# Attention with decay and two squared-ReLU layers: the opening's scores, decays and exponentials done in another way

## The chip, the cores and the metric

The kernel runs on one core of a Trainium2 chip. The metric is the device time of one execution in microseconds (us), the median of several executions. Five engines work side by side: TensorE (PE; its weight loads are PEld), VectorE (DVE), ScalarE (ACT), GpSimd (POOL), and SyncE (SP), which here issues nearly all transfers.

## The reference

Attention over 4 batches and 8 heads, 576 positions, head size 64, with a decay made from running sums of log f; then two layers without biases, each of width 512 and hidden width 2048, on 2304 tokens.

```python
scores = scale * np.matmul(q, k.transpose(0, 1, 3, 2))          # scale = 1/8
cum = np.cumsum(np.log(np.clip(f, 0.0001, 1.0)), axis=-1)
decay = cum[:, :, :, None] - cum[:, :, None, :]
scores = np.where(causal, -1e9, scores + decay)                 # causal: key after query
attn = np.exp(scores - np.max(scores, axis=-1, keepdims=True))
attn = attn / (np.sum(attn, axis=-1, keepdims=True) + 1e-09)
x = np.matmul(attn, v)                                          # to tokens x 512
x = square(relu(x @ w_in)) @ w_out                              # twice, with weights of their own
```

## The kernel before, in words

**The order of the work.** The program is straight-line code. Every piece of work is registered as `op(engine, duration, function, priority, dependencies, buffers)`, and `Plan.run` plays all of them through once with estimated durations, when the kernel is built. Whenever an engine comes free there, the ready operation of lowest priority number is taken, and it is emitted into that engine's queue at that place. On the chip each engine keeps this order, whatever the real durations are. `either(m, ...)` gives an operation two possible engines: by `m` it prefers one and falls back on the other (0 and 1), or is fixed to one (2 to 4). Where TensorE has nothing to do in the plan, before `wu` = 43.42 us, a filler product (L1442) is emitted; nothing reads its result. The numbers in `TUNE` are priorities and engine choices of this planner, so that a change of them reorders the whole program.

**The stages.** Positions are cut at 0, 64, 192 and so on. The *first part* (`first_part(y, ...)`, y = 0 and 1, two batches each) computes attention for positions 0 to 63; its 256 columns are the first group of tokens (group 0) of the first layer. *Pairs* of heads (`pair`, L644 to L694) do positions 64 to 191, *units* of one head (`unit`, L702 to L830) the rest. The first layer (`hidden`, L918 and L993) goes over groups of 256 tokens and 16 hidden tiles; its 16 weight tiles of 1 MB come in as two words for each number, are decoded on VectorE (L873, L875, L877), rounded on ScalarE (L890) and subtracted for the remainder (L894). The second layer (L1290, L1316) follows.

**The first part before.** One transfer for each y (L530) puts queries and keys of 16 heads into `room[y]`, on 64 partitions, 512 KB. The decay enters as two extra rows of the product: VectorE clips f, ScalarE takes the logarithm, VectorE scans 64 positions (`scan0`) and writes 8 and -8 times the sums (`times8`, L1407) into `a0`; two transfers for each y (L533) then copy these rows to partitions 64 and 65 of `room[y]`. The scores are 16 products of 66 rows for each y (L547). VectorE scales them by 1/8 and adds the mask (L553), takes the maximum (L556), GpSimd or VectorE subtracts it (L557), ScalarE takes one exponential of all 512 columns (L558), VectorE sums (L559), adds 1e-9 (L560), takes the reciprocal (L562), and VectorE or GpSimd multiplies (L563). Then come transposes (L575), a copy (L578), the products with the values (L587), and the split of the result into a rounded part and a remainder (L602, L604), from which group 0 of the first layer starts (L918).

**The transfers' order.** SP issues f, y = 0's queries and keys, the first half of weight tile 0, the decay rows of y = 0, y = 1's queries and keys and its decay rows, the second half of weight tile 0, the values, and weight tiles 1 and 2. All of these except the first three wait for `aug_first`, the end of `scan0`.

Of the kernel before, what the change touches and what calls it, by code (L numbers as in the profile page):

```python
# [19 lines left out]
Q0, QA = QB[1:3]  # L20
# [243 lines left out]
def attention_then_two_squared_relu_mlps(  # L264
# [102 lines left out]
    mask2 = ap_.tile([128, 1, Q0], BF16, name="mask2")  # L367
# [31 lines left out]
    room = [wp.tile([128, 2048], F32, tag="w", name="tmp") for _ in range(9)]  # L399
    WHOLE = Pool([st, ph_a.rearrange("p i n c -> p (i n c)").bitcast(F32)[:, 0:2048], room[3]])  # L400
# [118 lines left out]
    def first_part(y, prio):  # L519

        qk_ = room[y].rearrange("p (n z s) -> p n z s", n=2 * H, z=2)
# [19 lines left out]
        first_loads.extend(l2)  # L541
        l3 = op("SP", P.COPY[0], load_v, U + 4 + y, [aug_first], data=0.95)
# [1046 lines left out]
```

## Time and profile before

| | before |
|---|---|
| median of 3 runs (lowest to highest) | 943.73 us (942.67 to 945.62) |
| profiled execution, its own time | 946.69 us |
| its span in the trace | 944.9 us |
| PE busy | 927.1 us, 98% of the span |
| DVE busy | 694.8 us, 74% |
| ACT busy | 503.5 us, 53% |
| POOL busy | 178.5 us, 19% |
| mean DMA rate | 145 GB/s |

The page gives busy time over the span; it counts the filler products as busy. Durations of matmuls overlap, so that a group's sum can exceed its stretch; busy time of a stretch counts each moment once. The releaser of a wait is the event that came last.

### The profile page before, as it was taken

Reading aid. Unit: us, or ns where it says so; the run is one execution under the profiler, and the core shown is the slowest. Engines: PE = TensorE matmul, PEld = TensorE weight load, DVE = VectorE, ACT = ScalarE, POOL = GpSimd, SP = SyncE. Lnnn points to the kernel's source line nnn. Section 1 sums busy time; section 2 is a strip of 40 time slices with the busy share of each in tenths; the row PEclk is TensorE's granted clock in tenths of the full one; section 3 lists DMA queues with packets and bytes.
Section 4 is the critical chain, followed back from the end, with each engine's and each line's share of the span. In section 5 each row is a group of like instructions: output and inputs, shape, how many; then the busy total and the mean of one; then the engine's idle time right before and its main releaser. Section 6 shows DMA issues by size and latency. Waiting matters only on the chain.

```text
span 944.9 us, 16695 instructions
## 1 busy us (share of the span) xinstructions
PE 927.1 (98%) x6356; PEld 854.5 (90%) x6356; DVE 694.8 (74%) x1363; ACT 503.5 (53%) x1064; POOL 178.5 (19%) x144
## 2 busy tenths in 40 slices
PE   7899999999999999999999999999999999999997
PEld 3899999989999999999999998888989898989886
DVE  7999878888888888786476799896765455745453
ACT  3697799888888998986343662231411012301011
POOL 4021201112112111230101001221821015501010
PEclk7999999999999999999999999999999999999999
DMA  9878458667767757655376229743261211311113
GB/s 271 262 230 253 127 113 180 141 117 171 182 124 173 184 108 155 149 114 112 111 263 218 78 90 292 244 154 134 67 200 68 68 67 67 133 68 67 67 68 112
DMA packets 164288, 137.12 MB, mean 145 GB/s; under 512 B 120752, under 2 KB 140720, under 8 KB 162160
## 3 DMA queue, kind: packets, MB, share of 16 engines
q1 hardware_dynamic: 163952, 135.56, 52.0%
q8 instruction: 50, 0.82, 0.4%
q10 hardware_dynamic: 256, 0.49, 0.2%
q14 instruction: 30, 0.25, 0.1%
HBM read 90.32 MB, written 18.42 MB: 115 GB/s over the span
## 4 chain that ended last, share of the span: by engine, by line
PE 84%; DVE 6%; DMA 4%; ACT 3%; issue 2%; SPq 0%; POOLq 0%; POOL 0%; DVEq 0%; ACTq 0%
PE yp L993 18%; PE hp L918 18%; PE hp L1290 17%; PE bk L1316 13%; PE yp L1316 6%; PE bk L807 4%; PE bk L773 4%; DMA stage<-in_w_dram 2%; PE bk L644 1%; PE bk L683 1%; DMA qk<-aug_d 1%; DVE gt L943 1%; DVE ph L442 1%; PE bk L670 1%; DMA tmp<-tmp 0%
## 5 line engine op out<-in xcount | busy, mean ns | idle before, releaser
L993 PE MATMUL yp<-gt,w 128*128 128x256 f32 x1728 | 229.5, 281 | 0.1
L918 PE MATMUL hp<-xk,w 128*128 128x256 f32 x1728 | 227.3, 282 | 1.6 <-DVE w L894 1.6
L918 PEld LDWEIGHTS hp<-xk,w 128*128 128x128 f32 x1728 | 214.4, 189 | 2.1 <-DVE w L894 1.8
L993 PEld LDWEIGHTS yp<-gt,w 128*128 128x128 f32 x1728 | 214.5, 188 | 0.8 <-DVE gt L943 0.4
L1316 PE MATMUL bk<-w,g 128*128 128x512 f32 x576 | 148.6, 394 | 0.2 <-POOL g L1303 0.2
L1302 ACT CAST g<-r 128x768 fp32r<-128x768 f32 x47 | 39.3, 835 | 181.0 <-DVE r L1301 180.8
L1290 PE MATMUL hp<-w 128*128 128x384 f32 x630 | 124.0, 335 | 0.2
L1316 PEld LDWEIGHTS bk<-w,g 128*128 128x128 f32 x576 | 106.6, 188 | 17.6 <-POOL g L1303 0.6
L1290 PEld LDWEIGHTS hp<-w 128*128 128x128 f32 x630 | 111.8, 188 | 8.2 <-DVE t L1267 0.4
L421 ACT ACTIVATE pp<-pp,stat 128x448 f32<-128x448 f32 (+1 forms) x128 | 78.1, 611 | 11.9 <-DVE stat L413 11.1
L1267 DVE TENSOR_TENSOR r<-hp,st 128x384 f32<-128x384 f32 x62 | 34.5, 556 | 58.2 <-PE hp L1290 58.0
L442 DVE SCALAR_TENSOR_TENSOR ph<-pp,stat,ph 128x320 f16<-128x320 f32 (+2 forms) x96 | 69.0, 722 | 10.2 <-ACT ph L435 9.3
L1303 POOL TENSOR_TENSOR g<-r,g 128x768 fp32r<-128x768 f32 x19 | 35.1, 1848 | 217.5 <-ACT g L1302 217.5
L1290 PE MATMUL hp<-w,far 128*128 128x384 f32 x378 | 74.4, 335 | 0.0
L1316 PE MATMUL yp<-w,g 128*128 128x512 f32 x288 | 74.4, 393 | 0.0
L435 ACT ACTIVATE ph<-pp,stat 128x320 f16<-128x320 f32 (+2 forms) x96 | 63.7, 666 | 16.5 <-DVE stat L429 15.1
L1301 DVE SCALAR_TENSOR_TENSOR r<-r 128x768 f32<-128x768 f32 x47 | 70.9, 1508 | 1.4
L1290 PEld LDWEIGHTS hp<-w,far 128*128 128x128 f32 x378 | 67.3, 188 | 4.9
L927 ACT ACTIVATE sq<-hp 128x512 f32<-128x512 f32 x72 | 42.8, 594 | 52.6 <-PE hp L918 51.6
L413 DVE CUSTOM_DVE_ANT_0 pp<-bk,mask 128x448 f32<-128x448 f32 (+1 forms) x128 | 59.6, 475 | 7.9 <-PE bk L773 5.3
L1316 PEld LDWEIGHTS yp<-w,g 128*128 128x128 f32 x288 | 53.3, 188 | 8.5
L943 POOL TENSOR_TENSOR gt<-sq,gt 128x512 fp32r<-128x512 f32 x22 | 28.6, 1300 | 149.1 <-ACT gt L940 107.4
(181 smaller groups left out, 1243.7 us busy)
## 6 DMA issues: line engine op xcount, KB each, us to landing
w<-wo_d SPq DMA_DIRECT2D x48, 512.0 KB
stage<-in_w_dram SPq DMA_DIRECT2D x26, 512.0 KB
raw<-in_qk_dram SPq DMA_DIRECT2D x32, 288.0 KB
wo_d<-part SPq DMA_DIRECT2D x16, 512.0 KB
ph<-in_w_dram SPq DMA_DIRECT2D x7, 1024.0 KB
st<-in_w_dram SPq DMA_DIRECT2D x6, 1024.0 KB
vv<-in_v_dram SPq DMA_DIRECT2D x32, 160.0 KB
st<-in_v_dram SPq DMA_DIRECT2D x15, 256.0 KB
```

The source lines that it names most:

```text
L413: nc.vector.tensor_tensor_reduce(out=x[:rows, c0:c0 + wd], in0=src, in1=msk, scale=-0.125, scalar=3.0e38 if first else nmax[:rows, 5:6], o ...
L421: nc.scalar.activation(out=x, in_=x, func=AF.Exp, scale=-1.0, bias=nmax[:rows, t:t + 1], accum_out=ssum[:rows, t:t + 1])
L435: nc.scalar.activation(out=a, in_=x, func=AF.Copy, scale=r)
L442: nc.vector.scalar_tensor_tensor(out=flat[:rows, z:z + wd], in0=x, scalar=r, in1=flat[:rows, 128 * blk:128 * blk + wd], op0=ALU.mult, op1= ...
L918: nc.tensor.matmul(ps, lhsT=lt, rhs=rh, start=(k_ == 0 and c == 0), stop=(k_ == KD - 1 and c == 2))
L927: nc.scalar.activation(out=sq()[:, :c], in_=ps()[:, :c], func=AF.Relu)
L943: eng.tensor_tensor(out=gt[1]()[:, :c], in0=sq()[:, :c], in1=f32(gt[0]()[:, :c]), op=ALU.subtract)
L993: nc.tensor.matmul(yp[d // 2]()[:, d % 2], lhsT=lt, rhs=rh, start=(i == 0 and c == 0 and d % 2 == 0), stop=(i == NF - 1 and c == 2), skip_ ...
L1290: nc.tensor.matmul(ps()[:, 0:TH], lhsT=lt, rhs=rh, start=(k_ == 0 and c == 0), stop=(k_ == 1 and c == 2))
L1301: o = op("DVE", dvs(TU), lambda r=r: nc.vector.scalar_tensor_tensor(out=r(), in0=r(), scalar=0.0, in1=r(), op0=ALU.max, op1=ALU.mult), e0, ...
L1302: h = op("ACT", act(TU), lambda r=r, g=g: nc.scalar.copy(out=g()[:, 0], in_=r()), e0, [o], [r, g])
L1316: nc.tensor.matmul(bank(ob[c]), lhsT=g()[:, a, c * 128:(c + 1) * 128], rhs=rw()[:, b], start=(p == 0 and x == 0 and z == 0), stop=(p == NP ...
```

## The change

1. `room[0]` takes the queries and keys of both y in one transfer of 1 MB on 128 partitions (`load_first`), y = 0 on partitions 0 to 63, y = 1 on 64 to 127. It waits for nothing.
2. The rows of the decay are no longer copied by transfers. f's first 64 columns are loaded a second time to 32 further partitions (`f_again`), so that clip, logarithm and scan work on 64 partitions. Two operands are built: `dec_l` (which heads are odd, and 8 times the sums, masked by that) and `dec_r` (-8 times the sums, and ones, each head's in its own 64 columns). One product of 64 rows for each y adds the decay of all 16 heads to the bank (`decays_first`).
3. The causal mask, now -8e9 in float32, is put into the bank by a product with the identity (`causal_first`), which opens the accumulation. The scores (`sc`, 64 rows) are added last.
4. The maximum is taken from the bank, negated, and scaled by 1/8 on 16 numbers for each partition; ScalarE takes eight exponentials for each y, one for each head's 64 columns, with scale and bias in the instruction, and sums in its accumulator. The subtraction on GpSimd and the sum on VectorE go. The 1e-9, the reciprocal and the multiplication stay, the latter fixed to VectorE (`f4=2`).
5. The second half of weight tile 0, and weight tile 1, no longer wait for `aug_first`; the values wait for `o_scan`; `scan1` waits for `right` of y = 1.
6. `TUNE` changes in many places: starting priorities of pairs, weights and units; the duplicates `k_dup` from ACT alone to DVE or ACT and `q_dup` from DVE alone to ACT or DVE; `p_hi` and the pairs' `fold` from ACT alone to ACT or DVE; the remainder of the layer's inputs from POOL alone to DVE or POOL; the first group's squares prefer DVE.

```diff
 TUNE = dict(
-    AP0=0.0, AP1=212.5, BP0=1591.79, BP1=207.89, P10=10.74, P11=1.88, P20=26.33, P21=3.47, P30=37.43,
-    P31=1.59, P40=50.84, P41=6.35, PP=917.52, SP0=-14.46, SP1=155.02, WP0=-459.53, WP1=133.32, e3=12,
-    e6=6, ev=0, f3=3, f4=0, fa=2, fo=20.89, hl=1, kd=3, kl=3,
-    la=0.1, nbo=2, nph=2, npt=1, nqa=3, pha=0, phi=2, pq=-119.59, pz=12.35,
-    qd=2, ql=0, sqa=1, sqe=1, vd=9.14, vr=2, wf=0.59, wl=3, wn=1,
-    wq=2, ws=5, wu=43.42, xl=3
+    AP0=61.03, AP1=210.53, BP0=1681.68, BP1=210.41, P10=12.79, P11=2.22, P20=25.59, P21=3.7, P30=37.43,
+    P31=1.6, P40=54.31, P41=5.72, PP=956.68, SP0=44.13, SP1=155.02, WP0=-387.86, WP1=129.19, e3=12,
+    e6=6, ev=0, f3=3, f4=2, fa=1, fo=14.55, hl=1, kd=0, kl=3,
+    la=-0.07, nbo=2, nph=2, npt=1, nqa=3, pha=0, phi=0, pq=-106.66, pz=14.91,
+    qd=1, ql=0, sqa=1, sqe=0, vd=4.28, vr=2, wf=0.59, wl=3, wn=1,
+    wq=2, ws=5, wu=43.42, xl=0
...
-        qk_ = room[y].rearrange("p (n z s) -> p n z s", n=2 * H, z=2)
+        qk_ = room[0][64 * y:64 * y + 64].rearrange("p (n z s) -> p n z s", n=2 * H, z=2)
...
-        l1 = op("SP", P.COPY[0], load_qk, U + 1.6 * y, [aug_first] if y else [], data=2.5)
-        l2 = [op("SP", P.COPY[0], lambda r=r: load_aug(r), U + 1 + y, [aug_first], data=0.1) for r in range(2)]
...
-                nc.tensor.matmul(bk()[64 * h:64 * h + 64, c:c + Q0], lhsT=qk_[:66, n, 0], rhs=qk_[:66, n, 1],
-                                 start=True, stop=True, skip_group_check=True)
+                nc.tensor.matmul(bk()[64 * h:64 * h + 64, c:c + Q0], lhsT=qk_[:, n, 0], rhs=qk_[:, n, 1],
+                                 start=False, stop=True, skip_group_check=True)
+
+        def causal_first():
+            nc.tensor.matmul(bk()[:, 0:512].rearrange("p (n s) -> p n s", n=H), lhsT=ident, rhs=mask2.to_broadcast([128, H, Q0]),
+                             start=True, stop=False, skip_group_check=True)
+
+        def exps():
+            for n in range(H):
+                nc.scalar.activation(out=x[:, n], in_=bk()[:, n * Q0:n * Q0 + Q0], func=AF.Exp, scale=0.125, bias=st[:, 0, n], accum_out=st[:, 1, n])
+
+        def decays_first():
+            nc.tensor.matmul(bk()[:, 0:512], lhsT=dec_l.rearrange("p h s -> p (h s)"), rhs=dec_r[:, y].rearrange("p n s -> p (n s)"),
+                             start=False, stop=False, skip_group_check=True)
+
+        e = op("PE", 0.9, causal_first, prio, [o_m2], [bk])
+        e = op("PE", 0.9, decays_first, prio, [e, o_own, o_left, o_right[y]], [bk], rows=64)
+        e = op("PE", 1.24, sc, prio, [e, first_qk], [bk], rows=64)
...
-                   (deps if i else []) + ([aug_first] if i or z else []), [st], data=(5.0 if i == 0 else 3.4) / cuts if wide else 1.46)
+                   (deps if i else []) + ([aug_first] if i > 1 else []), [st], data=(3.6 if i == 0 else 3.4) / cuts if wide else 1.46)
...
+        def odd_heads():
+            for z in (0, nh_):
+                nc.vector.tensor_reduce(out=odd[z:z + nh_, :, 0], in_=ident[z:z + nh_, z:z + nh_].rearrange("p (j h) -> p h j", h=2),
+                                        op=ALU.add, axis=mybir.AxisListType.X)
+            nc.vector.tensor_copy(out=dec_l[0:nh_], in_=odd[0:nh_].to_broadcast([nh_, 2, Q0]))
+
+        def own_heads():
+            nc.scalar.copy(out=dec_r[nh_:].rearrange("p y n s -> p (y n) s"),
+                           in_=own[nh_:].rearrange("p y i b z -> p (y i b) z").to_broadcast([nh_, 2 * H, Q0]))
+
+        def left():
+            nc.vector.scalar_tensor_tensor(out=dec_l[nh_:], in0=cum(nh_).to_broadcast([nh_, 2, Q0]), scalar=8.0,
+                                           in1=odd[nh_:].to_broadcast([nh_, 2, Q0]), op0=ALU.mult, op1=ALU.mult)
+
+        def right(y):
+            nc.vector.scalar_tensor_tensor(out=dec_r[0:nh_, y], in0=cum(0).to_broadcast([nh_, H, Q0]), scalar=-8.0,
+                                           in1=own[0:nh_, y].rearrange("p i b z -> p (i b) z").to_broadcast([nh_, H, Q0]), op0=ALU.mult, op1=ALU.mult)
```

GpSimd builds the operands' constants at the start: `own` by a memset and four selects on 16 columns, then the identity and the mask (`consts2`). ScalarE copies `own` into `dec_r` once (`own_heads`, 1024 columns on 32 partitions).

## Rows read from the trace of the kernel before

**Rows 1.** Windows over the span: stretch, length, engines' busy time, PE clock, DMA share, GB/s.

```profile
0.00:2.60 2.60, 1.38 (x4) 0.56 (x5) 0.34 (x2) 1.49 (x2) 1.60 (x11) 1.00 0.15 38
2.60:12.80 10.20, 7.44 (x76) 4.15 (x75) 5.79 (x11) 3.47 (x7) 5.07 (x13) 0.83 0.94 258
12.80:27.40 14.60, 12.47 (x107) 6.39 (x107) 14.40 (x28) 5.81 (x15) 3.33 (x2) 0.77 1.05 333
27.40:33.60 6.20, 4.45 (x35) 4.02 (x32) 6.20 (x14) 4.49 (x10) 0.00 (x0) 0.97 0.92 284
33.60:60.00 26.40, 25.14 (x194) 23.41 (x195) 24.92 (x47) 20.68 (x58) 2.18 (x2) 0.94 0.72 231
60.00:900.00 840.00, 836.73 (x5759) 781.83 (x5759) 623.38 (x1239) 460.77 (x965) 162.34 (x115) 1.00 0.52 140
```

**Rows 2.** Windows of the filler products alone (L1442): PE and PEld busy time.

```profile
0.00:27.40 27.40, 14.32 (x36) 4.38 (x36) 0.81 0.92 277
```

**Rows 3.** Timeline of the first 34 us: start, length, engine, line, operation, idle before.

```profile
0.74 0.41 SPq L1352 DMA_DIRECT2D tmp<-in_f_dram  x1
...
3.20 0.28 DVE L1402 TENSOR_TENSOR_SCAN tmp<-tmp 32x64 f32<-32x64 f32 x1
...
7.69 0.69 DVE L873 TENSOR_SCALAR tmp<-st 128x512 uint32<-128x512 uint32 x1 [2.37 <-DMA st<-in_w_dram]
...
8.37 1.20 PE L547 MATMUL bk<-tmp 66*64 66x64 f32 x32 [2.08 <-DMA tmp<-tmp]
...
10.79 1.98 PE L547 MATMUL bk<-tmp 66*64 66x64 f32 x32 [0.68 <-DMA tmp<-tmp]
...
12.81 0.69 DVE L553 SCALAR_TENSOR_TENSOR tmp<-bk,mask 128x512 f32<-128x512 f32 x1 [1.65 <-PE bk L547]
...
25.73 1.81 PE L644 MATMUL bk<-qk_a 66*128 66x192 f32 x12
...
27.40 3.18 PE L918 MATMUL hp<-xk,w 128*128 128x256 f32 x24
...
33.64 2.50 PE L918 MATMUL hp<-xk,w 128*128 128x256 f32 x10 [1.56 <-DVE w L894]
```

**Rows 4.** Groups by line and shape, first 60 us, DVE and POOL: busy, mean ns.

```profile
L553 DVE SCALAR_TENSOR_TENSOR tmp<-bk,mask 128x512 f32<-128x512 f32 x2 | 1.4, 686 | 1.7 <-PE bk L547 1.7
...
L559 DVE TENSOR_REDUCE tmp<-tmp 128x8 f32<-128x512 f32 x2 | 1.4, 675 | 0.0
...
L563 DVE TENSOR_TENSOR tmp<-tmp 128x512 f32<-128x512 f32 x1 | 1.3, 1300 | 0.0
...
L560 DVE TENSOR_SCALAR tmp<-tmp 128x8 f32<-128x8 f32 x2 | 0.3, 157 | 0.0
...
L557 POOL TENSOR_TENSOR tmp<-tmp 128x512 f32<-128x512 f32 x2 | 2.5, 1267 | 5.9 <-DVE tmp L556 3.1 <-DVE tmp L560 2.8
L563 POOL TENSOR_TENSOR tmp<-tmp 128x512 f32<-128x512 f32 x1 | 1.8, 1841 | 3.8 <-DVE tmp L562 3.8
```

**Rows 5.** ACT: timeline around 31 us, and one group of the first 60 us.

```profile
31.11 0.45 ACT L421 ACTIVATE pp<-pp,stat 128x192 f32<-128x192 f32 x1
31.46 0.19 ACT L421 ACTIVATION_READ_ACCUMULATOR pp<-pp,stat 128x1 f32 x1
31.55 0.62 ACT L937 ACTIVATE sq<-sq 128x512 f32<-128x512 f32 x1
...
L558 ACT ACTIVATE tmp<-tmp 128x512 f32<-128x512 f32 x2 | 1.3, 630 | 10.0 <-POOL tmp L557 10.0
```

**Rows 6.** Windows over the opening, for granted clock and transfer rate (last number).

```profile
2.50:7.50 5.00, 3.79 (x10) 1.18 (x8) 2.43 (x6) 2.98 (x6) 3.47 (x11) 1.00 1.00 262
...
10.00:12.50 2.50, 1.82 (x33) 1.74 (x32) 1.12 (x2) 0.19 (x1) 1.04 (x1) 0.50 0.80 300
12.50:18.00 5.50, 4.51 (x20) 1.70 (x16) 5.16 (x10) 1.30 (x3) 1.49 (x1) 0.67 1.01 421
```

**Rows 7.** The chain that ended last, around 190 us: start, us, what.

```profile
188.88 6.31 DMA qk<-aug_d
```

More of the change, by code (lines that the diff above doesn't have):

```diff
@@ L399, in attention_then_two_squared_relu_mlps @@
     room = [wp.tile([128, 2048], F32, tag="w", name="tmp") for _ in range(9)]
+    mask2 = room[1][:, 1280:1280 + Q0].rearrange("p (n s) -> p n s", n=1)
+    dec_r = room[1][0:64, 0:1024].rearrange("p (y n s) -> p y n s", y=2, n=H)
+    dec_l = room[1][0:64, 1024:1152].rearrange("p (h s) -> p h s", h=2)
+    own = room[1][0:64, 1152:1168].rearrange("p (y i b z) -> p y i b z", y=2, i=H // 2, z=1)
+    odd = room[1][0:64, 1168:1170].rearrange("p (h z) -> p h z", h=2)
     WHOLE = Pool([st, ph_a.rearrange("p i n c -> p (i n c)").bitcast(F32)[:, 0:2048], room[3]])
@@ L556, in first_part @@
[L556 to L559 removed]
+            ("DVE", dve(512), lambda: nc.vector.tensor_reduce(
+                out=st[:, 2, :, 0], in_=bk()[:, 0:512].rearrange("p (n s) -> p n s", n=H), op=ALU.max, axis=mybir.AxisListType.X, negate=True)),
@@ L560, in first_part @@
+            ("DVE", 0.1, lambda: nc.vector.tensor_scalar(out=st[:, 0], in0=st[:, 2], scalar1=0.125, scalar2=None, op0=ALU.mult)),
+            ("ACT", H * 0.29, exps),
             ("DVE", 0.15, lambda: nc.vector.tensor_scalar(
@@ L1342, in attention_then_two_squared_relu_mlps @@
         nh_ = B * H
+        two_f = [room[6][0:2 * nh_, i * S:i * S + Q0] for i in range(3)]
         f_in, f_log, f_cum = (room[6][0:nh_, i * S:(i + 1) * S] for i in range(3))
@@ L1392, in f_clip @@
         def f_clip(a, z):
-            nc.vector.tensor_scalar(out=f_in[:, a:z], in0=f_in[:, a:z], scalar1=1.0e-4, scalar2=1.0, op0=ALU.max, op1=ALU.min)
+            x = f_in[:, a:z] if a else two_f[0]
+            nc.vector.tensor_scalar(out=x, in0=x, scalar1=1.0e-4, scalar2=1.0, op0=ALU.max, op1=ALU.min)
         def f_ln(a, z):
-            nc.scalar.activation(out=f_log[:, a:z], in_=f_in[:, a:z], func=AF.Ln)
+            x, y = (f_in[:, a:z], f_log[:, a:z]) if a else two_f[:2]
+            nc.scalar.activation(out=y, in_=x, func=AF.Ln)
         def tables():
@@ L1446, in attention_then_two_squared_relu_mlps @@
         o_f = o
-        o = op("DVE", dve2(Q0), lambda: f_clip(0, Q0), U, [o_f])
+        o_own = op("ACT", act(1024), own_heads, U, [o_c])
+        o_odd = op("DVE", 0.3, odd_heads, U, [o_m2])
+        o = op("DVE", dve2(Q0), lambda: f_clip(0, Q0), U, [o_f, o_again])
         o = op("ACT", act(Q0), lambda: f_ln(0, Q0), U, [o])
         o_f = op("DVE", dve2(S - Q0), lambda: f_clip(Q0, S), -1.0e7, [o_f])
-        o_f = op("ACT", act(S - Q0), lambda: f_ln(Q0, S), U, [o_f])
-        op("ACT", 1.5, lambda: nc.scalar.activation(out=stat[:, 0, 0, 6:7], in_=stat[:, 0, 0, 7:8], func=AF.Exp), U, [o_f])
-        aug_first = o = op("DVE", 0.55, scan0, U, [o, o_c])
+        o_f = op("ACT", act(S - Q0), lambda: f_ln(Q0, S), U, [o_f, o])
+        o = o_scan = op("DVE", 0.28, scan0, U, [o, o_c])
+        o_left = op("DVE", 0.24, left, U, [o, o_odd])
+        o_right = [op("DVE", dvs(512), lambda y=y: right(y), U, [o, o_c]) for y in range(2)]
+        aug_first = o_right[1]
         o_m1 = op("POOL", 2.5, consts1, U + 1, [o_m2, aug_first])
@@ L1455, in attention_then_two_squared_relu_mlps @@
         o_m = op("POOL", 1.3, consts, -1.0e7 + 1, [o_m1])
+        op("ACT", 1.5, lambda: nc.scalar.activation(out=stat[:, 0, 0, 6:7], in_=stat[:, 0, 0, 7:8], func=AF.Exp), U + 1.5, [o_f, aug_first])
         first_done, first_loads = [], []
@@ L1458, in attention_then_two_squared_relu_mlps @@
             first_part(y, -1.0e8 + y)
-        o = op("DVE", 1.62, scan1, -1.0e7, [o_f])
+        o = op("DVE", 1.62, scan1, -1.0e7, [o_f, o_right[1]])
         o_8 = op("ACT", 2 * act(QA), times8_act, -1.0e7, [o, o_m1])
```

52 lines of the change are left out of this document (23 added, 29 removed).

## The prediction

> **What bounds the kernel now.** I read the busy table first (TensorE 98%), then windows by stage, to see where the last 2% lie. From 60 to 900 us TensorE is busy for 836.73 of 840 us at the full clock [rows 1]; there the change, which leaves the products of pairs, units and layers as they are, can hardly win. What is lost lies in front. Up to 27.4 us TensorE is idle for 27.4 - 1.38 - 7.44 - 12.47 = 6.11 us [rows 1], and 14.32 us more go to filler products [rows 2]; from 27.4 to 60 us it is idle for another 1.75 + 1.26 us [rows 1]. So some 23 us can be won at most, and only in the opening.
>
> The timeline then shows what ends the opening. The first layer starts at 27.40 us [rows 3], when the first part of y = 1 is through. Its chain: decay rows land, scores 10.79 to 12.77 us, then 14.63 us of softmax, transposes, products with the values and splitting. The second thing to see is VectorE: idle for 4.41 of the 10.2 us up to 12.8 us, then busy for 14.40 of 14.60 and for all of the 6.20 us to 33.6 [rows 1], where TensorE stands for 1.56 us until VectorE has finished the third weight tile [rows 3]. So two clocks run side by side: the chain of y = 1, and VectorE's decoding of weights. The gain is what both allow.
>
> **The start of the scores.** Before, the scores of y = 0 start at 8.37 and those of y = 1 at 10.79 us, both after the transfers of the decay rows [rows 3]; these go, and the queries and keys themselves decide. In the trace before, 74 KB of f, 524 KB of queries and keys and 524 KB of weights had landed when VectorE began decoding at 7.69 us [rows 3]. The new order puts f, f's 8 KB again and 1049 KB of queries and keys ahead, the same 1.13 MB, starting one issue (0.41 us [rows 3], with its gap 0.45) later: 8.15 us. That is the mean rate of 262 GB/s between 2.5 and 7.5 us; at the 421 GB/s of 12.5 to 18 us [rows 6] the 1.05 MB would take 2.5 instead of 4.0 us: 6.65 us, the lower bound. The Trainium skill (SBUF — State Buffer, Door 1: The DMA port swizzle) says that a tile on partitions 0 to 63 reaches half of the ports, and gives 196 against 328 GB/s for 1 MiB on 64 and on 128 partitions; by that, as an estimate, 3.2 us and 7.35 us. No row here shows the two widths by themselves.
>
> The decay's operands: the scan ends at 3.48 us [rows 3], now 0.45 later at 3.93; then `left` (at most the scan's 0.28), and `right` twice at 0.69, the price of L553, another two-input operation on 512 columns [rows 4]: 5.6 us, or 6.1 if VectorE's counting of odd heads has to wait for GpSimd's longer list. TensorE then has four products of 512 float32 columns. The nearest row is two pairs' scores, 768 float32 columns in 1.81 us [rows 3], so 1.21 us each. The two mask products lie before the operands are ready; the two decay products end at 7.5 to 8.5 us. So transfer and operands come out nearly together, and scores start at 8.15 us (7.5 to 8.5). At 1.20 us each [rows 3], y = 1's are done at 10.55 instead of 12.77 us: 2.2 us won. The four products cost nothing beside filler; were the clock at its lower level, the scores would take the 1.98 us that y = 1's took [rows 3] at a granted clock of 0.50 [rows 6].
>
> **From the scores to the first layer.** Taken out of y = 1's 14.63 us: L553 0.69, L557 1.27, the exponential 0.63, the sum 0.68, GpSimd's multiplication 1.84 [rows 4, 5]; together 5.11. Put in: the scaling 0.16, VectorE's multiplication 0.69 [rows 4], and eight exponentials. One of 192 columns and its accumulator's reading take 31.55 - 31.11 = 0.44 us from start to start; 512 columns take 0.63 against 0.45 for 192, 0.00057 us a column [rows 5], so 64 columns take 0.44 - 128 x 0.00057 = 0.37 us, eight 2.9 us; the bounds are 0.44 each, 3.5, and one instruction's 0.63. The Trainium skill (ScalarE: Activation LUTs, What ACT_TABLE_LOAD costs) speaks against splitting: an activation with a pointer as bias takes about 280 ns plus 0.833 ns a column and overlaps the next by 93 ns. By that, an estimate, 0.24 us a head and 0.33 with the 0.09 us that the row shows for the reading: 2.6 us, and 0.6 us less over both halves. Both halves' exponentials queue on ScalarE: y = 0's run from 10.4 to 13.3 us, y = 1's are ready at 11.5 and wait 1.8 us. Sum: 14.63 - 5.11 + 0.16 + 0.69 + 2.9 + 1.8 = 15.1 us, from 10.55 to 25.65 us: 1.75 us won.
>
> That keeps every wait of before, and they were many, since VectorE was full: five of the chain's steps ran there, each coming up behind a decode step of 0.69 or 1.2 us. Half of such a step each, 1.7 to 3.0 us in all, is an estimate of it. After the change VectorE has less to do while ScalarE exponentiates (13.3 to 16.2 us), so part goes. The chain wins 1.75 us with all waits kept, 4.75 with none; I take 3.3.
>
> **VectorE's own sum.** Out: two L553, two sums, one multiplication at 1.30 [rows 4], the two small `times8`: 1.37 + 1.35 + 1.30 + 0.3 = 4.3 us. In: odd heads 0.5, `left` 0.28, `right` 1.38, two scalings 0.3, two multiplications 1.38: 3.8 us. The work hardly falls, by 0.5 us. What can be won is the idle 4.41 us: the holes of 2.37 us (first weights landing) and 1.65 us (scores of y = 1) [rows 3]. The first weights now land behind the larger transfer, about 2 us later, but the second half and tile 1 are right behind them and no longer wait for the scan; the remaining hole is that from `scan1`'s end (7.5 to 8) to the first maximum at 9.4. I take 2.3 of the 4.0 us as won, so 2.8 us in all, between 0.5 and 4.5. GpSimd's work leaves the stretch too: L563 on VectorE took 1.30 us for 512 columns beside it, L553 0.69 [rows 4].
>
> **Moved, and hidden.** Second half and tile 1 pass the values on SP's queue; these now land after some 3.75 MB, at 12 to 17 us by the two rates, where y = 0's product wants them at about 15.5: up to 1.5 us for y = 0, nothing for y = 1, which comes later. `scan1` and with it the pairs' decay store move from 5.3 to about 7.5 us; that store was issued after the values' and weights' transfers in any case. The table load for the exponentials follows the operands, 6.1 to 7.6 us, 2.8 us ahead of the first exponential. The new priorities touch everything from 60 us on, where VectorE is busy for 623 and ScalarE for 461 of 840 us [rows 1]; moves between them are covered there, and I cost them at nothing.
>
> **Sum.** The chain allows 3.3 us (1.75 to 4.75), VectorE 2.8 (0.5 to 4.5); TensorE fills part of the difference with pairs. I take 3.4 us. The profiled execution is 946.69 us for a span of 944.9, 3 us above the median of 943.73; against it 943.3, against the median **940.3 us**. Within 0.3%, 2.8 us (940.9 to 946.6), a measurement of this kernel can hardly tell a time from no change.
>
> **Rivals.**
> *More than the opening (0.14).* The new order also closes waits behind it: 1.75 + 1.26 us to 60 us, and the 3.27 us idle from 60 to 900 [rows 1], most of it where the first unit waits for a transfer at 188.88 us [rows 7]. With the chain's 4.75 and half of these 6.3 us: 7.9 us, 935.8. For it: these waits exist, and the pieces around them are reordered. Against: nothing in the change aims at them.
> *VectorE keeps the bound (0.14).* The hole is not filled, because weights land later behind the 1 MB; then 0.5 us, at most 1.5: 942.7. For it: 14.40 of 14.60 us busy [rows 1], and a work list hardly shorter.
> *The handover at 190 us widens (0.12).* The transfer on the chain lasts 6.31 us [rows 7], of which TensorE stands still for about 2 and works on other things for the rest. The duplicates' engines and the units' priorities change; with that cover gone, 4.4 us more: 944.7.
> *Slower: the first transfer shares its engines with the weights (0.08).* Before, y = 1's queries and the second half of tile 0 were held back until the scan. Now 2.1 MB of weights are issued right behind the 1.05 MB. If the engines serve them side by side, queries and keys land with the last of 3.2 MB, at 10.7 to 15.3 us by the two rates plus a microsecond. TensorE then stands after its four products, and works at the lower clock, as y = 1's scores did after the 2.08 and 0.68 us of idling before them [rows 3, 6]; scores at 1.98 us each end at 15.7 to 20.3 instead of 10.55 us, and the first layer starts 1.8 to 6.4 us later than now: 945.5 to 950.1. It is slower by more than 0.3% from a landing at about 12.8 us on. Against it: 1.12 MB had landed at 7.69 us though more was queued.
>
> **How the numbers follow.** The forecast has 0.52, its own range 937.7 to 942.3 (gains of 1.4 to 6 us). Faster by over 0.3%: 0.37 of it, all of the first rival, a little of the third: 0.53. Within: 0.14 of the forecast, nearly all of the second rival, half of the third: 0.33. Slower: the fourth and the rest of the third: 0.14. The range of 8 in 10 reaches from the first rival's 935 to 946.5, past the third's.
>
> **What would show it.** Scores of y = 0 at about 8.2 us without a hole after the decay products, at the full clock; exponentials at 0.37 us a head; the first L918 between 22.6 and 25.7 us; VectorE's idle time up to 12.8 us down from 4.41 to about 2; the third weight tile's products about 31 us. I am wrong if the first layer starts early but TensorE then stands until 60 us, if scores come after 12 us, or if the windows past 60 us hold other than 3.3 us of idling.

## The result and the profile after

The changed kernel takes **951.84 us** (median of 13 runs, 946.69 to 956.09) against 945.62 us of the kernel before in the same measurement (13 runs, 942.67 to 947.61): ratio **1.0055, 95% interval 1.0035 to 1.0074**. It is slower by about 5 us; 940.3 us were forecast, and the range ended at 946.5. The profiled execution, 956.09 us with a span of 954.4, is the longest of the 13. Its granted clock is 0.991, where the median of the 13 runs is 0.994 and the fastest run, 946.69 us, had 0.998; so its trace shows more loss to the clock than a typical run has. But the fastest run too is 4.0 us behind the fastest of the kernel before.

Windows over the span of the changed kernel, with the columns of [rows 1]:

```profile
0.00:2.60 2.60, 1.31 (x3) 0.28 (x3) 0.34 (x2) 1.77 (x3) 1.61 (x12) 1.00 0.10 31
2.60:12.80 10.20, 9.35 (x79) 4.29 (x79) 7.97 (x14) 3.64 (x7) 4.97 (x16) 1.00 0.98 366
12.80:27.40 14.60, 12.41 (x117) 7.02 (x115) 14.19 (x30) 10.18 (x46) 0.00 (x0) 0.88 0.89 280
27.40:33.60 6.20, 4.55 (x33) 4.35 (x32) 6.20 (x8) 4.77 (x7) 0.00 (x0) 0.91 0.75 229
33.60:60.00 26.40, 24.39 (x181) 23.23 (x180) 22.90 (x48) 16.38 (x47) 1.27 (x1) 0.89 0.67 208
60.00:900.00 840.00, 830.61 (x5729) 775.26 (x5728) 631.52 (x1252) 454.29 (x967) 158.82 (x110) 1.00 0.49 140
```

The opening did what was asked of it by these rows: VectorE idles for 10.20 - 7.97 = 2.23 us up to 12.8 us instead of 4.41, and TensorE for 4.33 us up to 27.4 us instead of 6.11. The loss lies behind it: from 60 to 900 us TensorE idles for 840 - 830.61 = 9.39 us, where it was 3.27 [rows 1], and from 33.6 to 60 us the granted clock is 0.89 where it was 0.94.

The fillers of the opening (window of that line alone, as in [rows 2]) fell from 14.32 to 11.70 us:

```profile
0.00:27.40 27.40, 11.70 (x38) 3.80 (x38) 0.94 0.85 289
```

TensorE's timeline, which answers to [rows 3] (L543 mask, L1478 filler, L551 decays, L539 scores, L923 first layer, L649 scores of pairs; of each mask, decay and score product the trace has two records):

```profile
1.29 1.46 PE L1478 MATMUL yp<-sq 128*128 128x512 bf16 x3 [1.29 <-DVE sq L1471]
3.60 3.78 PE L543 MATMUL bk<-tmp,ident 128*128 128x512 f32 x4 [0.85 <-POOL tmp L1374]
7.18 1.49 PE L1478 MATMUL yp<-sq 128*128 128x512 bf16 x3
8.59 1.98 PE L551 MATMUL bk<-tmp 64*128 64x512 f32 x4
10.50 1.91 PE L539 MATMUL bk<-tmp 64*64 64x64 f32 x64
...
19.02 1.49 PE L1478 MATMUL yp<-sq 128*128 128x512 bf16 x3
...
24.17 1.47 PE L1478 MATMUL yp<-sq 128*128 128x512 bf16 x6
25.29 3.80 PE L923 MATMUL hp<-xk,w 128*128 128x256 f32 x26
30.74 1.45 PE L923 MATMUL hp<-xk,w 128*128 128x256 f32 x10 [1.65 <-DVE w L899]
32.02 2.79 PE L649 MATMUL bk<-qk_a 66*128 66x192 f32 x12
```

The scores stand at 10.50, not 8.15 us, but without a hole before them, so they did not wait for the transfer; and both y are done at 12.41 us in 1.91 us. The first layer starts at 25.29 us, 2.11 us earlier. At 30.74 us TensorE still stands for 1.65 us for the third weight tile.

TensorE gained much less than these 2.11 us. Before, two pairs' scores stood ahead of the first layer, 1.81 us at 25.73 [rows 3]; here fillers stand there, and the same scores come at 32.02 us, behind it. Windows of those products alone, the pairs' scores before and the first layer after, give what was done by 27.4 us:

```profile
0.00:27.40 27.40, 1.67 (x12) 1.62 (x12) 0.81 0.92 277
0.00:27.40 27.40, 1.99 (x14) 1.72 (x14) 0.94 0.85 289
```

That is 0.3 us ahead of the kernel before.

The pace of the first products needs care. The granted clock reads 1.00 from 0 to 12.8 us, but three fillers took 1.46 us at 1.29 and 1.49 us at 7.18. So they did at 19.02 us, where the granted clock was 0.50, the level of 1.2 GHz; at 24.17 us, where it was 1.00 (2.4 GHz), six of them took 1.47:

```profile
19.00:20.50 1.50, 1.50 (x9) 0.36 (x7) 1.50 (x3) 1.23 (x2) 0.00 (x0) 0.50 0.95 368
24.00:25.20 1.20, 1.20 (x23) 0.61 (x14) 1.20 (x3) 0.93 (x5) 0.00 (x0) 1.00 0.88 335
```

So the fillers on either side of the mask products, and with them the mask, ran at half pace, whatever that column says. The trace before has the same: twelve fillers from 1.22 us took 5.07 us, 0.42 each, where [rows 6] read 1.00. Two mask products took 3.78 us and two decay products 1.98. In e3 (below) the fillers still took 0.53 us each just ahead of the decays, and the decays took 3.78 as well; so the difference is the pace, and not 128 rows against 64:

```profile
7.17 1.06 PE L1477 MATMUL yp<-sq 128*128 128x512 bf16 x2
8.16 3.78 PE L550 MATMUL bk<-tmp 64*128 64x512 f32 x4
```

VectorE and ScalarE in the same stretch, from the timeline: the two `right` (L1444), the first decoding, the first maximum (L561), and the first head's exponential and the next one's start:

```profile
4.86 1.28 DVE L1444 SCALAR_TENSOR_TENSOR tmp<-tmp 32x512 f32<-32x512 f32 x2
...
8.35 1.72 DVE L878 TENSOR_SCALAR tmp<-st 128x512 uint32<-128x512 uint32 x1 [0.76 <-DMA st<-in_w_dram]
...
11.70 0.69 DVE L561 TENSOR_REDUCE tmp<-bk 128x8 f32<-128x512 f32 x1 [0.68 <-PE bk L539]
```

```profile
13.17 0.31 ACT L548 ACTIVATE tmp<-bk,tmp 128x64 f32<-128x64 f32 x1 [4.87 <-DVE tmp L563]
13.38 0.19 ACT L548 ACTIVATION_READ_ACCUMULATOR tmp<-bk,tmp 128x1 f32 x1
13.47 0.30 ACT L548 ACTIVATE tmp<-bk,tmp 128x64 f32<-128x64 f32 x1
```

And what TensorE waits for between 60 and 900 us (line, what it waited for, us in total, times, longest):

```profile
PE bk L649 <- DVE stat L417: 2.7, 1, 2.7
PE hp L923 <- DVE xk L975: 1.6, 1, 1.6
PE bk L649 <- issue: 1.4, 1, 1.4
PE bk L778 <- DVE stat L417: 1.2, 3, 0.8
PE bk L778 <- DVE up_down L507: 0.8, 1, 0.8
```

The wait for the transfer at 190 us [rows 7] is gone; in its place are waits for VectorE. The longest shows how they come about. VectorE's timeline ahead of it, TensorE's next product, and the windows behind it:

```profile
77.09 1.77 DVE L975 TENSOR_TENSOR xk<-X,xk 128x512 fp32r<-128x512 f32 x1
78.79 1.21 DVE L882 SCALAR_TENSOR_TENSOR tmp<-ph,tmp 128x1024 uint32<-128x1024 uint32 x1
79.93 0.15 DVE L433 RECIPROCAL stat<-stat 128x2 f32<-128x2 f32 x1
80.00 0.33 DVE L417 CUSTOM_DVE_ANT_0 pp<-bk,mask 128x192 f32<-128x192 f32 x1
```

```profile
80.67 1.86 PE L649 MATMUL bk<-qk_a 66*128 66x192 f32 x6 [2.68 <-DVE stat L417]
```

```profile
60.00:80.00 20.00, 17.74 (x145) 16.07 (x143) 17.52 (x32) 14.17 (x37) 3.15 (x2) 1.00 0.84 233
80.00:85.00 5.00, 4.33 (x19) 4.33 (x20) 4.67 (x11) 4.01 (x11) 0.00 (x0) 0.52 0.74 249
85.00:87.00 2.00, 2.00 (x13) 1.66 (x12) 1.27 (x6) 0.00 (x0) 0.00 (x0) 0.50 0.01 2
```

A remainder of the layer's inputs (L975), which the new choices let VectorE take, and a decode step (L882), 3 us together, stand in VectorE's queue ahead of the pair's mask and maximum (L417). TensorE needs the bank that L417 frees, stands for 2.68 us, and works at half the clock (0.52 and 0.50 granted, the level of 1.2 GHz) for the next 6. VectorE was busy for 17.52 of 20 us, so not all the time; what held TensorE up is the order of its queue.

The books of the two profiled executions, behind 27.4 us: TensorE idles 0.65 us longer to 60 us and 6.12 us longer from 60 to 900. Up to 100 us the clock takes 6.9 instead of 1.6 us (length times what is missing to a granted clock of 1, windows of 27.4 to 60 and 60 to 100 us). The kernel before loses another 1.7 us to it behind its wait for the transfer at 190 us:

```profile
195.00:205.00 10.00, 9.67 (x64) 8.43 (x65) 6.69 (x18) 7.43 (x19) 1.29 (x1) 0.83 0.40 80
```

So the clock takes 3.6 us more. Against this stand the 0.3 us of products done by 27.4 us. 0.65 + 6.12 + 3.6 - 0.3 = 10.1 us, where the spans differ by 954.4 - 944.9 = 9.5.

### The profile page after: what moved, and what is told of

It is laid out like the page before. It is cut to its first block, busy times and chain, and to the rows that moved or that the text cites. A ratio compares the mean times of both kernels' runs of the same rounds, so it can differ in the third digit from the quotient of the medians.

```text
span 954.4 us, 16749 instructions
## 1 busy us (share of the span) xinstructions
PE 931.5 (98%) x6366; PEld 856.9 (90%) x6366; DVE 707.6 (74%) x1380; ACT 498.7 (52%) x1085; POOL 172.2 (18%) x141
## 4 chain that ended last, share of the span: by engine, by line
PE 72%; DVE 12%; DMA 6%; ACT 5%; issue 4%; POOL 0%; POOLq 0%; ACTq 0%; SPq 0%; DVEq 0%
PE hp L1295 17%; PE yp L998 14%; PE hp L923 13%; PE bk L1321 13%; PE yp L1321 6%; DMA stage<-in_w_dram 3%; PE bk L812 3%; PE bk L778 3%; DMA ph<-in_w_dram 3%; DVE ph L446 2%; DVE pp L417 1%; ACT pp L425 1%; DVE tmp L880 1%; DVE tmp L882 1%; ACT sq L932 1%
## 5 line engine op out<-in xcount | busy, mean ns | idle before, releaser
L923 PE MATMUL hp<-xk,w 128*128 128x256 f32 x1728 | 226.4, 281 | 3.5 <-DVE w L899 1.6
L923 PEld LDWEIGHTS hp<-xk,w 128*128 128x128 f32 x1728 | 213.0, 189 | 4.8 <-DVE w L899 2.2
L446 DVE SCALAR_TENSOR_TENSOR ph<-pp,stat,ph 128x320 f16<-128x320 f32 (+2 forms) x96 | 71.4, 745 | 9.6 <-ACT ph L439 8.4
L417 DVE CUSTOM_DVE_ANT_0 pp<-bk,mask 128x448 f32<-128x448 f32 (+1 forms) x128 | 59.5, 476 | 6.4 <-PE bk L675 2.3
L439 ACT ACTIVATE ph<-pp,stat 128x448 f16<-128x448 f32 (+2 forms) x74 | 48.3, 655 | 16.2 <-DVE stat L433 15.4
```

The costliest lines, as they stand in the source:

```text
L417: nc.vector.tensor_tensor_reduce(out=x[:rows, c0:c0 + wd], in0=src, in1=msk, scale=-0.125, scalar=3.0e38 if first else nmax[:rows, 5:6], o ...
L439: nc.scalar.activation(out=a, in_=x, func=AF.Copy, scale=r)
L446: nc.vector.scalar_tensor_tensor(out=flat[:rows, z:z + wd], in0=x, scalar=r, in1=flat[:rows, 128 * blk:128 * blk + wd], op0=ALU.mult, op1= ...
L923: nc.tensor.matmul(ps, lhsT=lt, rhs=rh, start=(k_ == 0 and c == 0), stop=(k_ == KD - 1 and c == 2))
```

## The experiments

"Old numbers" are the `TUNE` of before, "new numbers" that of the change. Ratios are to the kernel before on the same chip. Idle is TensorE's, and clock what the granted clock took from 27.4 to 100 us; both, like the first layer's start, are from each kernel's one profiled execution, in us. One execution is a thin base: e18 keeps before's order and time, but idles for 2.56 us from 200 to 600 us where before idles for 0.60. In more than half of the kernels a single product stands at the first layer's start and the next ones come later (in e17 at 26.05 us), so that this column tells little of TensorE's gain.

| kernel | ratio (95% interval) | first layer | idle 60 to 200 | idle 200 to 600 | clock |
|---|---|---|---|---|---|
| before | 1 | 27.40 | 2.68 | 0.60 | 1.6 |
| after | 1.0055 (1.0035 to 1.0074) | 25.29 | 5.02 | 4.37 | 6.9 |
| e1 new code, old numbers | 0.9972 (0.9950 to 0.9994) | 24.89 | 2.32 | 1.76 | 0 |
| e2 old code, new numbers | 1.0069 (1.0043 to 1.0095) | 27.55 | 3.64 | 5.58 | 0 |
| e3 e1 with new engine choices | 1.0210 (1.0164 to 1.0255) | 27.91 | 4.87 | 10.06 | 2.4 |
| e4 e1 with new priorities | 1.0043 (1.0021 to 1.0064) | 23.74 | 2.35 | 5.78 | 0 |
| e5 after, folds and squares back | 1.0006 (0.9981 to 1.0031) | 25.33 | 4.53 | 4.51 | 0 |
| e6 after, units' numbers back | 1.0096 (1.0068 to 1.0123) | 23.68 | 2.38 | 6.23 | 1.6 |
| e7 e1, units' numbers new | 1.0048 (1.0031 to 1.0065) | 26.05 | 2.05 | 4.20 | 1.6 |
| e8 e1, weights held back | 0.9968 (0.9955 to 0.9980) | 25.46 | 0.86 | 1.77 | 0 |
| e9 after, squares back | 1.0030 (1.0011 to 1.0049) | 23.67 | 2.54 | 4.48 | 0 |
| e10 after, folds back | 1.0050 (1.0026 to 1.0075) | 25.46 | 1.91 | 4.87 | 0 |
| e11 e8, one exponential | 1.0097 (1.0065 to 1.0128) | 24.17 | 3.40 | 4.47 | 3.3 |
| e12 e8, folds and squares new | 1.0001 (0.9985 to 1.0017) | 22.11 | 3.58 | 1.20 | 3.6 |
| e13 e1, priorities mirrored | 1.0066 (1.0040 to 1.0092) | 24.48 | 4.83 | 4.18 | 3.3 |
| e14 e1, priorities half way | 1.0000 (0.9984 to 1.0017) | 25.75 | 2.91 | 2.74 | 0 |
| e15 before, exponentials alone | 1.0064 (1.0042 to 1.0085) | 26.30 | 2.40 | 4.67 | 6.2 |
| e16 e1, units' choices new | 1.0058 (1.0036 to 1.0081) | 24.61 | 3.82 | 6.76 | 0 |
| e17 e11 in e8's order | 0.9947 (0.9928 to 0.9966) | 24.17 | 0.43 | 1.75 | 1.6 |
| e18 e15 in before's order | 1.0006 (0.9982 to 1.0030) | 27.84 | 1.86 | 2.56 | 4.6 |

**The code or the numbers (e1, e2).**

```diff
 e1: in after
-    AP0=61.03, AP1=210.53, BP0=1681.68 and so on: the whole TUNE
+    AP0=0.0, AP1=212.5, BP0=1591.79 and so on
 e2: in before, the other way round
```

> The changed code of the opening with all planner numbers and engine choices of before. Theory O (the loss sits in the new numbers, which order the weight loads, pairs and units; the opening itself wins some 2 us): 940 to 944 us, 2 to 5 us under the kernel before, last weight tile rounded before 100 us. Theory C (the new opening itself sets the rest back, whatever the numbers): 948 to 953 us, last weight tile rounded at 105 us or later.

> The code of before with all planner numbers and engine choices of the change. Theory O: slower than the kernel before by 5 to 9 us (the changed kernel's loss without its gain in the opening), 950 to 954 us. Theory C: as the kernel before within 2 us, 944 to 947 us.

The new code with the old numbers is faster, by 0.06 to 0.5%; the new numbers make even the old code slower by 0.69%, with much of the idle time where the change has it, 5.58 us from 200 to 600 us. The numbers cost what the new code won, and more. e1 is not the opening alone, though: the new code gives the planner other operations, so that e1's order differs from before's as well.

**Choices or priorities (e3, e4).**

```diff
 e3: in e1
-    f4=0, fa=2, kd=3, phi=2, qd=2, sqe=1, xl=3
+    f4=2, fa=1, kd=0, phi=0, qd=1, sqe=0, xl=0
 e4: in e1
-    f4=0 and 20 old priorities, AP0 to vd
+    f4=2 and 20 new ones
```

> The changed code with the old priorities, and the new engine choices (duplicates, fold, first group's squares, remainders of the inputs towards VectorE). If within theory O it is the work moved onto VectorE that costs: as the changed kernel or slower, 949 to 954 us, with VectorE waits of TensorE between 200 and 600 us as in the changed kernel (about 4 us idle there). If it is the priorities: as e1, 940 to 944 us.

> The changed code with the new priorities and the old engine choices. If it is the priorities that hold back the weight tiles from the sixth on: 949 to 954 us, last weight tile rounded at 104 to 107 us. If it is the engine choices: as e1, 940 to 944 us.

The halves do not add up: against the kernel before, the choices lose 2.1%, the priorities 0.43%, both together 0.55%. The choices alone leave TensorE idle for 10.06 us from 200 to 600 us, and the clock at half (0.53 granted) from 306 to 317 us. That the priorities hold back the weight tiles fell: e4's last one is rounded at 95.6 us, the change's at 106.5.

**Folds and squares (e5, e9, e10, e12).**

```diff
 e5: in after (e9: sqe alone; e10: fa alone)
-    fa=1, sqe=0
+    fa=2, sqe=1
 e12: in e8
-    fa=2, sqe=1
+    fa=1, sqe=0
```

> The changed kernel with two engine choices back: the pairs' fold on ScalarE alone, the first group's squares preferring ScalarE. Theory W (VectorE decodes the weight tiles, and the fold and squares that the new choices put there stretch the time from tile to tile from 5.6 to 6.2 us): last weight tile rounded at 95 to 100 instead of 106.5 us, TensorE's idle time from 60 to 100 us down from 2.9 to under 2 us; 947 to 950 us. Rival N (the numbers as a whole, no single one): last tile still after 103 us, 950 to 955 us.

> The changed kernel with one number put back: the squares again divided as before (sqe=1). Undoing the folds and the squares together had brought the ratio from 1.0055 to 1.0006, and nearly all of the 7.0 us between the two spans was clock (3.3 + 3.6 us lost between 27.4 and 100 us against none). Theory 1, the folds carry it (VectorE stands at a fold until TensorE has the product, and the weight tiles' decoding queues behind it): this run stays at 1.003 to 1.007, with the clock falling below full again between 27.4 and 100 us. Theory 2, the squares carry it: 0.999 to 1.002 and no clock lost there. Theory 3, each carries half: 1.002 to 1.004.

> The changed kernel with the other number put back: all folds on ScalarE again (fa=2), the squares as changed. Theory 1, the folds carry it: 0.999 to 1.002, no clock lost between 27.4 and 100 us, TensorE idle there as in the run with both back (6 us). Theory 2, the squares carry it: 1.003 to 1.007. Theory 3, each carries half: 1.002 to 1.004.

> The best version so far (0.9968) with the two numbers of the folds and the squares as the change has them (fa=1, sqe=0): the opposite test of undoing them in the changed kernel, which was worth 0.5% there. If these two are bad in themselves: 1.0005 to 1.003, with clock lost between 27.4 and 100 us and the last first-layer weight tile some 4 us later than 96.86. If they are bad only together with the moved units: 0.996 to 0.999, no clock lost and the last tile within 2 us of 96.86.

Both back are worth 0.5%, and the clock's loss is gone; the last weight tile comes at 98.6 us, as theory W had it. But TensorE's idle time from 60 to 100 us, which W wanted under 2 us, stayed at 3.08 (2.94 in the change). The squares alone give 0.25% and the folds alone 0.05%, with intervals that overlap the unmended kernel's, and no theory had both figures. My theory that the folds carry it, because VectorE stands at them, fell. The clock of one trace does not settle the time either: e10 lost none from 27.4 to 100 us and was hardly faster than the change.

In the best version the two numbers cost 0.33%, between the two bands, and the trace repeats the change's picture between 60 and 100 us: two pairs' scores wait for VectorE's L416 (L417 in the change), and the clock lies at half behind that.

```profile
72.51 0.71 PE L687 MATMUL bk<-pt,vv 128*128 128x128 f32 x4 [0.71 <-ACT pt L677]
74.16 2.71 PE L648 MATMUL bk<-qk_a 66*128 66x192 f32 x12 [0.68 <-DVE stat L416]
```

```profile
75.00:80.00 5.00, 5.00 (x24) 5.00 (x24) 5.00 (x7) 3.14 (x12) 0.00 (x0) 0.50 0.98 284
```

**The units' numbers (e6, e7, e16).**

```diff
 e7: in e1 (e6: in after, the other way round; e16: in e1, the second line alone)
-    BP0=1591.79, BP1=207.89, P10=10.74, P11=1.88, P20=26.33, P21=3.47, P31=1.59, P40=50.84, P41=6.35
-    kd=3, qd=2, phi=2, xl=3
+    BP0=1681.68, BP1=210.41, P10=12.79, P11=2.22, P20=25.59, P21=3.7, P31=1.6, P40=54.31, P41=5.72
+    kd=0, qd=1, phi=0, xl=0
```

> The changed kernel with the units' part of the numbers back as before (starting points of units and their loads, engines of the duplicates, of the upper parts and of the inputs' remainders); the numbers of weights and pairs stay new. Theory U (the idle 4.4 us between 200 and 600 us come from the units' numbers): idle there under 2 us, last weight tile unchanged near 106 us, 947 to 950 us. Rival N: idle there still 4 us or more, 950 to 955 us.

> The opposite test: new opening, all numbers of before, except the units' part, which is the change's. Theory U: last weight tile as with the old numbers (98 us), idle between 200 and 600 us 4 to 6 instead of 1.8 us; 948 to 951 us. Rival N: as with all old numbers, 944 to 946 us.

> New opening and old numbers (0.9972) with four of the units' engine choices as in the change (kd, phi, qd, xl), their priorities as before; with the priorities too it was 1.0048 and TensorE idled 4.2 us from 200 to 600 us instead of 1.8. Theory 1, the choices carry it: 1.003 to 1.007, idle 3.5 us or more there. Theory 2, the priorities carry it: 0.996 to 0.999, idle 1 to 2.5 us there. Theory 3, neither by itself, the pair: 0.999 to 1.002.

Put into e1 these numbers cost 0.76%, as expected; taken out of the change they should have given that back, and it became slower instead (four runs), with 6.23 us idle from 200 to 600 us. By themselves the choices cost as much as with their priorities. So no group of numbers "carries" the loss: most steps away from the old numbers cost. Nor does the late last weight tile: in e6 it is rounded at 98.7 us, where the change has 106.5, and e6 is the slower of the two.

**Weights held back (e8).**

```diff
-(deps if i else []) + ([aug_first] if i > 1 else [])
+(deps if i else []) + ([aug_first] if i or z else [])
```

> New opening, all numbers of before, but the second half of weight tile 0 and tile 1 wait for the decay's operands again, as before the change. If the early weights carry the opening's gain (VectorE's idle time filled with decoding): first layer's second weight tile later by 2 to 4 us, 947 to 949 us, gain over the kernel before gone. If the shorter chain to the first layer carries it: within 1 us of the same kernel with early weights, 944.5 to 946.5 us.

The earlier weights carry nothing of e1's gain that these runs can tell: held back as before, the kernel is as fast (0.9968). The test is not quite pure, since this edit moves the order too (about an eighth of the entries, counted as below).

**Any step of the numbers? (e13, e14).**

```diff
 in e1, for each of the 20 priorities
-    old
+    2 * old - new        (e13)
+    (old + new) / 2      (e14)
```

> New opening, before's engine choices, and each of the 20 changed priorities moved from its old value by the same step as in the change, but the other way. The old priorities gave 0.9972 here, the changed ones 1.0043 (one engine choice apart). Theory 1, any step of this size away from the old numbers costs about as much, because the order of the instructions was fitted to them: 1.002 to 1.008, with TensorE idle 3 us or more from 200 to 600 us. Theory 2, the changed numbers are bad in their direction: 0.994 to 0.999.

> The same, with each of the 20 priorities half way between its old and its changed value. Theory 1, an order fitted to the old numbers that any step spoils: 1.001 to 1.006, not in proportion to the step. Theory 2, a smooth cost of the direction: 0.9995 to 1.002, half way between 0.9972 and 1.0043.

The opposite step is as bad, 1.0066, with 4.18 us idle from 200 to 600 us. The half step, 1.0000, costs 0.28% against e1: by its median theory 2's figure, though its interval reaches theory 1's. So in these four points the cost rises on both sides of the old numbers, and on the side of the new ones with the step: a valley, with the old numbers near its floor. It is not the direction alone that is wrong with the new numbers.

**A small edit of the softmax (e11, e15), and the same edit with the order held (e17, e18).** The code is shortened here.

```diff
 e11, e17: in e8
-            ("ACT", H * 0.29, exps),
+            ("DVE", dve(512), x = bk * 0.125 + st[:, 0]),
+            ("ACT", act(512), x = exp(x)),
+            ("DVE", dve(512), st[:, 1] = sum(x)),
 e15, e18: in before
-            ("f3", subtract), ("ACT", act(512), exp), ("DVE", dve(512), sum),
+            ("ACT", H * 0.29, exps),
 e17, e18: in Plan.run
+                        if o.prio[1] != head[e]:     # next of a list written out
+                            continue                 # by the unedited kernel's plan
```

> The best version so far (new opening, old numbers, weight tiles held until the decays; ratio 0.9968) with the softmax of the first part done as before: maximum, one scale-and-subtract on VectorE, one exponential of 512 columns on ScalarE, sums by VectorE, instead of eight exponentials with accumulated sums. Mask and decays stay products. Theory 1, the per-head exponentials buy little, since ScalarE's pitch of 0.29 us a head (2.3 us a half) stands where one exponential and two VectorE passes stood (0.6 + 2 x 0.65 us): 0.996 to 0.9985, first layer at 25.5 to 26.5 us. Theory 2, they carry most of the opening's gain by freeing VectorE: 0.9985 to 1.001, first layer at 26.5 us or later, VectorE idle before 12.8 us no less than in the best version.

> The kernel before with one part of the change alone: eight exponentials a half with the maximum as bias and accumulated sums, in place of the subtraction, one exponential and VectorE's sum; opening, mask, loads and numbers as before. Theory 1, the part is near neutral in itself (2.3 us of ScalarE against 0.66 + 0.6 + 0.65 us) and the plan hardly moves: 0.997 to 1.001, first layer between 26.4 and 27.6 us. Theory 2, it is what made the opening faster: 0.994 to 0.997, first layer before 26 us. Theory 3, the moved plan costs more than the part: 1.003 to 1.012 with the first layer no later than 27.6 us and the loss past 60 us.

> The kernel of e11 (best version with one exponential a half; 1.0097) with the order of the instructions on each engine held as in the best version itself (0.9968); apart from the edited instructions and six more fillers the two then give every engine the same sequence. Theory 1, the moved order carried e11's loss: 0.997 to 1.000, TensorE idle from 200 to 600 us back at 1 to 2.5 us. Theory 2, the exponentials in one piece carry it: 1.006 to 1.011.

> The kernel of e15 (before with eight exponentials a half; 1.0064) with the order on each engine held as in the kernel before; apart from the edited instructions and twelve fewer fillers the sequences are the same. Theory 1, the moved order carried e15's loss: 0.997 to 1.001, TensorE idle from 200 to 600 us at 0.5 to 2 us. Theory 2, the exponentials carry it: 1.004 to 1.009.

e11 came out where no theory had it, 1.3% behind e8, and e15 where its third had it, at 1.0064, though the edited instructions are over by 25 us. With the order held the same edits cost nothing that can be told: 0.9947 against 1.0097, and 1.0006 against 1.0064. That is theory 1 both times; e17 came out below its band, and e18 idled for 2.56 us from 200 to 600 us, where 0.5 to 2 were expected and e15 had 4.67. How much the plan moves can be counted in the traces: engine by engine, in order of start, the entries (some 9,000 in all) by operation, tiles, shape and source line. About a third have no match at their place between after and before, between e11 and e8, and between e13 and e1, somewhat more between e1 or e15 and before, and a quarter between e14 and e1. Between e17 and e8, and between e18 and before, it is under 1%, the edited instructions included.

The windows of e11, where the order moved:

```profile
60.00:100.00 40.00, 37.37 (x308) 34.71 (x309) 35.79 (x63) 31.67 (x87) 5.34 (x4) 1.00 0.72 227
100.00:200.00 100.00, 99.23 (x801) 93.90 (x800) 84.99 (x223) 87.98 (x211) 23.41 (x24) 1.00 0.59 145
200.00:600.00 400.00, 395.53 (x3131) 377.83 (x3130) 312.75 (x708) 276.14 (x581) 55.21 (x43) 1.00 0.57 153
```

and of e17, with the same instructions in e8's order:

```profile
60.00:100.00 40.00, 39.58 (x330) 37.13 (x328) 38.75 (x78) 34.85 (x98) 6.56 (x4) 1.00 0.80 244
100.00:200.00 100.00, 99.99 (x815) 95.54 (x815) 83.77 (x219) 88.42 (x206) 20.06 (x23) 1.00 0.56 138
200.00:600.00 400.00, 398.25 (x3141) 381.27 (x3140) 317.06 (x704) 278.48 (x582) 67.00 (x52) 1.00 0.61 161
```

TensorE's idle time from 60 to 600 us is 2.63 + 0.77 + 4.47 = 7.87 us in the one and 0.42 + 0.01 + 1.75 = 2.18 us in the other. e17 is the fastest kernel of the study; it, e1 and e8 are faster than the kernel before and the changed one. Its interval overlaps that of e8.

## Why the prediction was wrong

**The opening: near in size, but not by the forecast's way.** The gain forecast was 3.4 us. With the old numbers the new code won 0.28% (e1) and 0.32% (e8), 2.7 and 3.0 us. The chain to the first layer did become shorter, as below. But it was costed as if TensorE gained what the chain does, and TensorE had filled the end of the wait with two pairs' scores; only 0.3 us more were done by 27.4 us in the change, and in e1 0.5 (2.16 us of first-layer products). e1's profiled span is 3.6 us shorter than before's (941.3 against 944.9). Its idle time from 27.4 to 900 us is not shorter (6.9 against 6.3 us); what is gone are the 1.6 and 1.7 us that the clock took before, and e1's granted clock is 1.00 from 27.4 to 900 us. So in this trace the forecast's size came about mostly by the clock, which the sum did not hold: that it came near is in good part luck. And as e1's order is another than before's, how much is the opening's own stays open.

- *Start of the scores.* Forecast 8.15 us (7.5 to 8.5), measured 10.50. The transfer and `right` were in time (`right` ended at 6.14 us, and weights queued behind the transfer were being decoded at 8.35). Mis-sized were the mask products: 1.21 us each was read from pairs' scores at the full clock, and they took 1.89, at the half pace of the fillers around them. The decays behind took 0.99. The sign "at the full clock" thus failed for the mask, though [rows 6] had read 1.00 there. And three fillers, 1.4 us, stood between mask and decays, since the plan puts an idle TensorE there.
- *The scores.* 2.40 us for both were forecast, 1.91 measured, so both were done at 12.41 instead of 10.55 us: 0.36 us won where 2.2 were forecast.
- *The chain behind.* 12.9 us to the first layer (12.41 to 25.29), between the 15.1 with all waits kept and the 12.1 with none that were forecast. A head's exponential comes every 0.29 us, not 0.37: the 0.37 was drawn from longer ones. The Trainium skill (ScalarE: Activation LUTs, What ACT_TABLE_LOAD costs), with an estimate of 0.33 us by its figures and the accumulator's reading, was nearer than the row, and still above it.
- *VectorE.* Idle up to 12.8 us: about 2 forecast, 2.23 measured. First layer: 24.1 (22.6 to 25.65) forecast, 25.29 measured. Third tile's products: about 31, measured 30.74.

That the exponentials belong to the gain was assumed and fell: e17 with one exponential is no slower than e8 with eight, and e18 has them alone, at 1.0006. What is left of the opening is the other way to the scores' sum, mask and decays by products and without the copies of the decay rows; by itself it was not tested.

**The rest: the step that failed** is "The new priorities touch everything from 60 us on, where VectorE is busy for 623 and ScalarE for 461 of 840 us [rows 1]; moves between them are covered there, and I cost them at nothing." They cost about 0.8% (e1 to after), some 8 us. Cover was argued from mean busy time, VectorE 623 of 840 us. But in queues that keep the order written by a plan, what counts is what stands directly ahead of the one instruction that TensorE needs: VectorE was 88% busy from 60 to 80 us, and its queue held TensorE up for 2.68 us. The prediction's own test, other than 3.3 us of idling past 60 us, was met with 9.39 us.

**The rivals.** None of them was this. The handover at 190 us did not widen, the wait there vanished; the first transfer did not hold the scores up; VectorE's hole was filled. "Slower" was given 0.14, for the first transfer and for half of the handover rival, the one place where new engines and priorities were given a price. That a new order of a third of all entries could be worse throughout than one that leaves 3.27 us idle in 840 was missing: 3.27 us can be won there, but far more can be lost.

**How far it is settled.** Shown: the loss is in the numbers (e1, e2), and orders alone cost 0.6 to 1.5% (e11 against e17, e15 against e18; e13, which has e1's instructions but for a few on the other of their two engines). Of the loss in the change itself, waits behind VectorE's queue and the clock after them are read from its one trace, that of its slowest run. That squares and folds start the clock's part is likely: e5 has 6.9 us of clock and 4.6 us of time less, the median granted clock of its ten runs is 0.998 against 0.994 in the change's, and in the opposite test e12 such a wait and the half clock come back between 60 and 100 us. Against it stands e10, and the two halves e9 and e10 are too close to tell apart. Which numbers cost the rest is open. After's own instructions in an order of the old kind were not run.

## What to carry to other kernels

Where a planner writes the order of the whole program, an edit is two edits: price the instruction and the reshuffle, and hold the order fixed to tell them apart. A program that is 99.6% busy past its opening has little to win there and much to lose, so new planning numbers deserve a cost and a chance for slower, even when all engines but one have slack. For slack, don't read mean busy time; read what stands ahead of the instruction that the bound engine waits for. And when a chain gets shorter, count the useful work that the bound engine did while it waited for the old one: that part is not won.

## What the runs showed of the hardware

A hole on TensorE cost more than its length. After 1.65 us of idling before 30.74 us and after 2.68 us before 80.67 us the granted clock lay at half speed for more than 6 us each time (6.9 us lost in all). The first of the two, and the stretch behind it:

```profile
33.60:39.00 5.40, 5.40 (x27) 5.40 (x26) 5.40 (x13) 1.65 (x6) 0.00 (x0) 0.50 0.84 269
39.00:60.00 21.00, 18.99 (x156) 17.83 (x155) 17.50 (x38) 14.73 (x41) 1.27 (x1) 0.99 0.63 193
```

Not each hole did that: 1.35 us before 43.55 us left the clock at 0.99. Nor was a long hole needed: in e12 the clock lay at 0.50 from 75 to 80 us behind holes of 0.71 and 0.68 us. And runs of one program differ by it: the changed kernel took 946.69 us at a mean clock of 0.998 and 956.09 at 0.991. In the first microseconds the granted clock read 1.00 while fillers took 0.49 us each, as long as at 0.50. A product of 64 rows and 512 float32 columns took 0.99 us in the change and 1.89 in e3, as long as one of 128 rows at that pace.
